# Attention and MLP on one Trainium2 core: a new order for the first batch of attention heads, another order of its loads, and the last result in two halves

## The chip, the cores and the metric

The kernel runs on one core of one Trainium2 chip. The metric is device time in microseconds (us) of one execution. Most numbers below are medians of several runs; the profile of one run gives the span (first to last instruction, some 1.7 us shorter than the time). The runs here are called slow when they are over 1.5% above the fastest of the same kernel, and the others fast.

## The reference, cut to what matters

```python
batch, n_heads, seq, head_dim = 8, 8, 576, 64
scores = q @ k.T / sqrt(64);  cum = cumsum(max(s, 0))
scores = where(causal, -1e9, scores + min(-(cum_i - cum_j), 0))
attn   = softmax(scores)
x      = (attn @ v) as [4608 tokens, 512]        # all heads of a token side by side
h      = x @ w_in                                 # 512 -> 2048
out    = (h * clip(h + 3, 0, 6) / 6) @ w_out      # 2048 -> 512, fp32 out
```

Nothing of the MLP for a batch can start before all eight heads of that batch are through. So the first batch, heads 0 to 7 (pairs 0 to 3), stands alone at the start of the kernel; every later batch is woven into the MLP of an earlier one.

## The kernel before: the parts that matter

In the traces, TensorE's matmuls and VectorE's instructions stand in the order in which the program issues them: in one pass before, VectorE's copies, division, cast of v and next copies start at 25.48, 26.51, 27.50 and 28.16 us. The work of a pair of heads goes round the engines like this (cuts are marked):

```python
def transpose_group(p, g):              # q and k of pair p: PE transposes, then VectorE
    ...                                 # 5 or 4 PE transposes into one PSUM bank
    for dst, r0 in ((qT, 0), (kT, 64)):
        nc.vector.tensor_copy(out=dst[...], in_=pT[...])           # L262
def cast_v(p):                          # on VectorE for p < 4
    copy(out=v_h[:, sl, :, :, 0:D], in_=v_f[:, sl])                # L238
def scores_bank(hd, bi):                # four banks a head
    nc.tensor.matmul(out=S, lhsT=kT[...], rhs=qT[...])             # L291
    nc.scalar.activation(out=P, in_=S, func=AF.Exp)                # L299
    nc.gpsimd.affine_select(...)        # causal mask                L304
def attend(hd):                         # "values"
    nc.tensor.matmul(out=O, lhsT=P[...], rhs=v_h[...])             # L340, 15 of them
    if hh == 1:                         # second head of the pair: divide
        nc.vector.reciprocal(...); nc.vector.tensor_tensor(out=xs, ...)   # L350, L352
def x_transpose(p):                     # output transposes of the pair
    nc.tensor.matmul(out=pX, lhsT=xs[...], rhs=ident, is_transpose=True)  # L378
    nc.vector.tensor_copy(out=xT[...], in_=pX)                     # L386
```

The order of the first batch before (one pass per pair p):

```python
scores(2p)
if p == 1: cast_v(0); load_v(3); load_aug(3); ...; attend(0)
transpose_group(p + 1, 0)               # p < 3
attend(2p - 1)                          # p > 0
scores(2p + 1)
cast_v(p)                               # p > 0
cast_qk(p + 2)                          # p < 2, on GpSimd
transpose_group(p + 1, 1)
x_transpose(p - 1); attend(2p)          # p > 0
... after the last pass: keep_warm(4); attend(7); x_transpose(3); first projection (L423)
```

The softmax here doesn't subtract the row's maximum and nothing guards it: scores larger than these inputs give would overflow.

## Time and profile before

| | before |
|---|---|
| median time | 376.63 us of 3 runs (375.51 to 377.32) |
| span of the profiled run | 374.9 us, mean granted clock 0.994 |
| first projection starts | 35.56 us |
| last matmul ends | 370.86 us (367.24 + 3.62) |

The first projection splits the kernel: up to there the engines hand small pieces to one another, after it TensorE is nearly full (busy 327.87 of the 335.30 us to the end of the last matmul).

### The profile page before, as it was taken

What the parts mean: (1) busy time and instruction counts of PE and PEld (TensorE: products, weight loads), DVE (VectorE), ACT (ScalarE), POOL (GpSimd) and SP (SyncE); (2) the same over time, 40 slices, a digit from 0 to 9 for tenths busy, and PEclk for the clock granted to TensorE, in tenths of its full rate; (3) what the DMA queues carried; (4) which work ended last, traced back from release to release, by engine and by line L of the source; (5) the groups of instructions that cost most, each with busy time, mean ns of one, the idle gap of its engine ahead of it and who ended that gap; (6) DMA issues with size and microseconds to landing.
All of it is one profiled execution on the core that took longest, in us unless ns stands there. A gap on an engine that the chain in (4) does not pass through costs nothing.

```text
span 374.9 us, 7607 instructions
## 1 busy us (share of the span) xinstructions
PE 354.1 (94%) x2784; PEld 219.6 (59%) x2784; DVE 190.9 (51%) x331; ACT 209.5 (56%) x404; POOL 148.9 (40%) x378
## 2 busy tenths in 40 slices
PE   6688979999999999999999999999999999999995
PEld 2465555556666566566656665666566656555542
DVE  5765855566652365345534553455345545554531
ACT  4464764336785677467746774677467714543310
POOL 5663335453666444444444444444445300000000
PEclk9989999999999999999999999999999999999999
DMA  9679999949799999998998989899995100010012
GB/s 161 138 155 203 191 212 211 229 118 194 147 205 204 231 219 198 202 235 189 187 235 180 199 183 233 191 191 185 219 188 113 49 29 36 22 56 30 28 58 84
DMA packets 184526, 59.36 MB, mean 158 GB/s; under 512 B 177840, under 2 KB 178064, under 8 KB 184488
## 3 DMA queue, kind: packets, MB, share of 16 engines
q1 hardware_dynamic: 182392, 54.42, 69.5%
q0 software_dynamic: 1680, 4.27, 6.3%
q8 instruction: 22, 0.36, 0.4%
q10 hardware_dynamic: 416, 0.19, 0.2%
q14 instruction: 16, 0.13, 0.1%
HBM read 37.49 MB, written 9.62 MB: 126 GB/s over the span
## 4 chain that ended last, share of the span: by engine, by line
PE 79%; DMA 8%; DVE 5%; ACT 4%; issue 2%; SPq 1%; POOL 1%; ACTq 0%; POOLq 0%
PE bank L423 25%; PE po L445 23%; PE S L291 9%; PE bank L445 8%; PE O L340 6%; PE bankS L423 4%; DMA qkT<-xb 3%; DMA qkT<-aug_scratch 3%; ACT Pm L299 2%; DMA qkf<-in_k_dram 1%; ACT trl L431 1%; DVE gT L432 1%; PE bank L465 1%; DMA s_sb<-in_s_dram 1%; DVE xs L352 1%
## 5 line engine op out<-in xcount | busy, mean ns | idle before, releaser
L299 ACT ACTIVATE Pm<-S 128x384 f16<-128x384 f32 (+2 forms) x256 | 115.5, 507 | 58.8 <-PE S L291 57.1
L432 DVE SCALAR_TENSOR_TENSOR gT<-trl,bank 128x512 f16<-128x512 f32 x123 | 84.5, 687 | 102.2 <-ACT trl L431 102.0
L304 POOL TENSOR_SCALAR_AFFINE_SELECT Pm<-Pm 128x128 f16<-128x128 f16 (+2 forms) x256 | 79.2, 311 | 132.6 <-ACT Pm L299 121.9
L431 ACT ACTIVATE trl<-bank,bias 128x512 f32<-128x512 f32 x123 | 85.2, 693 | 77.3 <-PE bank L423 75.3
L423 PE MATMUL bank<-xT,w_in 128*128 128x512 f16 x492 | 126.4, 382 | 0.7
L445 PE MATMUL po<-w_out_sb,gT 128*128 128x512 f16 x416 | 104.3, 379 | 0.0
L423 PEld LDWEIGHTS <-w_in 128*128 128x128 f16 x576 | 78.5, 146 | 32.9 <-issue 1.9
L445 PEld LDWEIGHTS <-gT 128*128 128x128 f16 x576 | 52.2, 98 | 48.6 <-issue 0.3
L291 PE MATMUL S<-qkT 128*128 128x320 f16 (+4 forms) x448 | 70.4, 263 | 8.0 <-ACT Pm L299 3.4
L291 PEld LDWEIGHTS <-qkT 128*128 128x128 f16 x448 | 41.3, 98 | 38.4 <-DVE qkT L262 4.5
L340 PEld LDWEIGHTS <-Pm 128*128 128x128 f16 x960 | 38.9, 98 | 13.2 <-POOL Pm L304 1.8
L340 PE MATMUL O<-v_h,Pm 128*128 128x65 f16 x960 | 41.4, 194 | 1.5 <-POOL Pm L304 1.3
L445 PE MATMUL bank<-w_out_sb,gT 128*128 128x512 f16 x160 | 39.4, 379 | 0.0
L352 DVE TENSOR_TENSOR xs<-O,r 128x640 f16<-128x640 f32 x32 | 26.4, 825 | 1.1
L454 DVE TENSOR_SCALAR osb<-po 128x512 f32<-128x512 f32 x26 | 17.9, 688 | 15.2 <-PE po L445 14.9
L222 POOL CAST xb<-qkf 128x1152 f16<-128x1152 f32 x22 | 25.3, 1149 | 0.0
L238 POOL CAST v_h<-v_f 128x640 f16<-128x640 f32 x28 | 20.1, 719 | 4.2 <-DMA v_f<-in_v_dram 4.2
L454 DVE TENSOR_SCALAR osb<-bank 128x512 f32<-128x512 f32 x10 | 6.9, 690 | 26.0 <-PE bank L445 26.0
L176 POOL CAST t<-qkf 128x1152 f16<-128x1152 f32 x10 | 11.5, 1146 | 13.1 <-DMA qkf<-in_k_dram 13.1
L423 PE MATMUL bankS<-xT,w_in 128*128 128x512 f16 x64 | 16.4, 379 | 0.0
L431 ACT ACTIVATE trl<-bankS,bias 128x512 f32<-128x512 f32 x16 | 11.0, 687 | 8.0 <-PE bankS L423 8.0
L432 DVE SCALAR_TENSOR_TENSOR gT<-trl,bankS 128x512 f16<-128x512 f32 x16 | 11.0, 689 | 6.8 <-ACT trl L431 6.8
(49 smaller groups left out, 122.7 us busy)
## 6 DMA issues: line engine op xcount, KB each, us to landing
qkf<-in_q_dram SPq DMA_DIRECT2D x32, 288.0 KB, 4.4
qkf<-in_k_dram SPq DMA_DIRECT2D x32, 288.0 KB, 4.1
out_dram<-osb SPq DMA_DIRECT2D x36, 256.0 KB, 2.7
v_f<-in_v_dram SPq DMA_DIRECT2D x64, 128.0 KB, 3.8
w_in<-in_moe_w_in_dram POOLq DMA_DIRECT2D x2, 1024.0 KB, 12.9
w_out_sb<-in_moe_w_out_dram POOLq DMA_DIRECT2D x4, 512.0 KB, 7.2
v_f<-in_v_dram SPq DMA_DIRECT2D x32, 32.0 KB, 2.7
qkT<-xb SPq DMA_TRANSPOSE x22, 4.9
```

What stands on the lines that cost most here:

```text
L222: nc.gpsimd.tensor_copy(out=x.rearrange("p (i t) c -> p t i c", i=2)[:, :, :, 0:D], in_=qk_f.pop(p))
L238: copy(out=v_h[:, sl, :, :, 0:D], in_=v_f[:, sl])
L291: nc.tensor.matmul(out=S[:, c:c + hi - lo], lhsT=kT[:, sl, off + 128 * kt:off + 128 * (kt + 1)], rhs=qT[:, sl, off + lo:off + hi], start=( ...
L299: nc.scalar.activation(out=P[:, p0:p0 + n], in_=S[:, 0:n], func=AF.Exp, scale=0.125, bias=0.0)
L304: nc.gpsimd.affine_select(out=view, in_=view, pattern=pattern, compare_op=ALU.is_ge, fill=0.0, base=0, channel_multiplier=-1,)
L340: nc.tensor.matmul(out=O[:, hh, qt * VW:qt * VW + D + 1], lhsT=P[:, c:c + 128], rhs=v_h[:, sl, hh, kt, 0:D + 1], start=(qt == 0), stop=(qt ...
L352: nc.vector.tensor_tensor(out=xs.rearrange("p t h d -> p h t d"), in0=Ov[:, :, :, 0:D], in1=r.to_broadcast([128, 2, 5, D]), op=ALU.mult,)
L423: nc.tensor.matmul(out=ph, lhsT=w_in_t[f // 8][:, kc, f % 8, :], rhs=xT[:, kc, n * 512:(n + 1) * 512], start=(kc == 0), stop=(kc == KC - 1),)
L431: nc.scalar.activation(out=trl, in_=ph, func=AF.Relu, bias=bias3[:, 0:1], scale=1.0)
L432: nc.vector.scalar_tensor_tensor(out=gT[n][:, f, :], in0=trl, scalar=6.0, in1=ph, op0=ALU.min, op1=ALU.mult)
L445: nc.tensor.matmul(out=po, lhsT=gT[n][:, f, t4 * 128:(t4 + 1) * 128], rhs=w_out_sb[:, f, :], start=(f == 0), stop=(f == NF - 1),)
L454: nc.vector.tensor_scalar_mul(out=osb, in0=po, scalar1=1.0 / 6.0)
```

## The change

Its intent: values two heads behind the scores, so that TensorE never waits for the causal masks; both groups of transposes of the next pair together; q and k of pair 3 loaded ahead of v of pairs 1 and 2; in each later load the small rows (`load_aug`) first. A second part, outside the first batch, computes the very last 128x512 result in two halves of 256 columns, the second evicted by ScalarE and sent by its queue.

```diff
 def load_pair(p):
+    if p < PTD: load_aug(p, nc.sync)
     load_qk(p, nc.sync); load_v(p, nc.sync)
-    if p < PTD: load_aug(p, nc.sync)
...
+for p in range(4):
+    run(scores(2 * p))
+    if p == 0:
+        transpose_group(1, 0)
+    else:
+        if p < 3:
+            transpose_group(p + 1, 0)
+            transpose_group(p + 1, 1)
+        cast_v(p - 1)
+        ...                                  # p == 1: load_v(3), load_aug(3), store_aug(1)
+        attend(2 * p - 2)
+    run(scores(2 * p + 1))
+    if p == 0:
+        transpose_group(1, 1)
+    else:
+        attend(2 * p - 1)
+        x_transpose(p - 1)
+    ...                                      # cast_qk(p + 2), w_in loads, load_pair(p + 2)
+cast_v(3)
+attend(6)
...
+load_qk(3, nc.sync)
 load_v(1, nc.sync)
+load_v(2, nc.sync)
...
+def last_result(n, t4):                      # replaces the last 128x512 result
+    for half, eng in enumerate((nc.sync, nc.scalar)):
+        ... 16 matmuls of 256 columns, evicted by VectorE (half 0) or ScalarE (half 1),
+        ... eng.dma_start(out=out[...], in_=osb[...])
```

More of the change, by code (lines that the diff above doesn't have):

```diff
@@ L443, in m2 @@
         po = pouts[n, t4]
+        if (n, t4) == (NBLK - 1, 3):
+            if part == 3:
+                last_result(n, t4)
+            return
         for f in range(4 * part, 4 * part + 4):
@@ L456, in m2 @@
             nc.sync.dma_start(out=out[r0:r0 + 128, :], in_=osb)
+    def last_result(n, t4):
+        r0 = n * 512 + t4 * 128
+        osb = work.tile([128, 512], F32, tag="osb", bufs=3)
+        for half, eng in enumerate((nc.sync, nc.scalar)):
+            c0, c1 = half * 256, (half + 1) * 256
+            po = pouts[n, t4] if half == 0 else psum.tile([128, 512], F32, tag="Y", name="poL")
+            for f in range(NF):
+                nc.tensor.matmul(
+                    out=po[:, 0:256],
+                    lhsT=gT[n][:, f, t4 * 128:(t4 + 1) * 128],
+                    rhs=w_out_sb[:, f, c0:c1],
+                    start=(f == 0),
+                    stop=(f == NF - 1),
+                )
+            if half == 0:
+                nc.vector.tensor_scalar_mul(out=osb[:, c0:c1], in0=po[:, 0:256], scalar1=1.0 / 6.0)
+            else:
+                nc.scalar.mul(out=osb[:, c0:c1], in_=po[:, 0:256], mul=1.0 / 6.0)
+            eng.dma_start(out=out[r0:r0 + 128, c0:c1], in_=osb[:, c0:c1])
     bias3 = cpool.tile([128, 1], F32, tag="c_b3")
@@ L492, in load_pair, with first_batch @@
     def load_pair(p):
+        if p < PTD:
+            load_aug(p, nc.sync)
         load_qk(p, nc.sync)
         load_v(p, nc.sync)
-        if p < PTD:
-            load_aug(p, nc.sync)
     def scores(hd):
         return [(lambda bi=bi: scores_bank(hd, bi), 400) for bi in range(4)]
-    def first_tasks(p):
-        def loads():
+    def first_batch():
+        for p in range(4):
+            run(scores(2 * p))
             if p == 0:
-                load_qk(3, nc.sync)
-                load_v(2, nc.sync)
-            elif p > 1:
-                load_pair(p + 2)
-        def v_first():
-            cast_v(0)
-            load_v(3, nc.sync)
-            load_aug(3, nc.sync)
-            store_aug(1, NA, 2 * PTD, nc.sync)
-        def casts():
-            if p > 0:
-                cast_v(p)
+                transpose_group(1, 0)
[4 more added lines that the diff above has]
+                cast_v(p - 1)
+                if p == 1:
+                    load_v(3, nc.sync)
+                    load_aug(3, nc.sync)
+                    store_aug(1, NA, 2 * PTD, nc.sync)
+                attend(2 * p - 2)
+            run(scores(2 * p + 1))
+            if p == 0:
+                transpose_group(1, 1)
+            else:
+                attend(2 * p - 1)
+                x_transpose(p - 1)
             if p < 2:
@@ L525, in casts @@
                 load_w_in(1)
-        tr = [[], []]
-        if p < 3:
-            tr = [[(lambda: transpose_group(p + 1, 0), 640)],
-                  [(lambda: transpose_group(p + 1, 1), 512)]]
-        t = scores(2 * p)
-        if p == 1:
-            t += [(v_first, 0), (lambda: attend(0), 1200)]
-        t += tr[0]
-        if p > 0:
-            t += [(lambda: attend(2 * p - 1), 1200)]
-        t += scores(2 * p + 1) + [(casts, 0)] + tr[1]
-        if p > 0:
-            t += [(lambda: x_transpose(p - 1), 640)]
-            t += [(lambda: attend(2 * p), 1200)]
-        return [(loads, 0)] + t
+            if p > 1:
+                load_pair(p + 2)
+        cast_v(3)
+        attend(6)
     pause = [(lambda: None, 1000)]
@@ L667 @@
         load_aug(p, nc.sync)
+    load_qk(3, nc.sync)
     load_v(1, nc.sync)
+    load_v(2, nc.sync)
     cast_qk(1)
     keep_warm(12)
-    for p in range(4):
-        run(first_tasks(p))
+    first_batch()
     load_pair(6)
```

## The prediction

> **What bounds the kernel now.** I read first the page's busy rows in 40 slices, to see where TensorE is not full.
>
> ```profile
> PE   6688979999999999999999999999999999999995
> ...
> PEclk9989999999999999999999999999999999999999
> ```
>
> One slice is 374.9 / 40 = 9.4 us. From slice 8 on TensorE is full at the full clock, so work there costs what it costs. The holes are in the first seven slices, some 66 us, and in the last. The rewritten order concerns the "first batch" (heads 0 to 7), so I read TensorE's own timeline next; columns are start, length, work, and in brackets the idle time before it and what ended it.
>
> ```profile
> 17.35 0.71 PE L291 MATMUL S<-qkT 128*128 128x256 f16 x6 [1.56 <-DMA qkT<-aug_scratch]
> 18.25 0.30 PE L291 MATMUL S<-qkT 128*128 128x320 f16 x1 [0.19 <-ACT Pm L299]
> 18.39 0.80 PE L340 MATMUL O<-v_h,Pm 128*128 128x65 f16 x15
> 19.00 0.72 PE L247 MATMUL pTm<-ident,t 128*128 128x128 f16 x5
> 19.52 1.03 PE L340 MATMUL O<-v_h,Pm 128*128 128x65 f16 x15
> ...
> 25.00 0.45 PE L247 MATMUL pTm<-ident,t 128*128 128x128 f16 x5 [0.87 <-POOL t L176]
> ...
> 33.46 0.63 PE L340 MATMUL O<-v_h,Pm 128*128 128x65 f16 x15
> 35.27 0.45 PE L378 MATMUL pT<-ident,xs 128*128 128x128 f16 x5 [1.17 <-DVE xs L352]
> 35.56 1.95 PE L423 MATMUL bank<-xT,w_in 128*128 128x512 f16 x8
> ```
>
> The batch runs from 12.7 us to 35.56 us, where the first projection (L423) begins; from there TensorE has few holes. The start of L423 is therefore what this part of the change moves. TensorE has short waits, each on ScalarE, VectorE or a transfer; none is on the causal masks of GpSimd, which "two heads back" would remove. The exponentials (L299) are 16 + 8 + 8 instructions of 0.50, 0.60 and 0.46 us, 16.5 us for eight heads, and ScalarE sits idle 6.0 us between them. So ScalarE could be a floor, but the handovers are what is paid now.
>
> Third, VectorE's timeline, because values (L340) need its cast of v (L238), scores need its copies of the transposes (L262), and the output transposes (L378) need its division (L350, L352).
>
> ```profile
> 25.48 0.99 DVE L262 COPY qkT<-pTm 64x640 f16<-64x640 f16 x2 [1.82 <-PE pTm L247]
> 26.51 0.22 DVE L350 RECIPROCAL r<-O 128x10 f32<-128x10 f32 x1
> 26.76 0.82 DVE L352 TENSOR_TENSOR xs<-O,r 128x640 f16<-128x640 f32 x1
> 27.50 0.73 DVE L238 CAST v_h<-v_f 128x640 f16<-128x640 f32 x1
> 28.16 0.85 DVE L262 COPY qkT<-pTm 64x512 f16<-64x512 f16 x2
> 29.04 0.46 DVE L386 COPY xT<-pTm 128x576 f16<-128x576 f16 x1
> ```
>
> In the kernel before, only one of the two copy pairs stands ahead of a cast, and the division is covered by scores and transposes.
>
> Fourth, windows of 1 us (the columns I use are TensorE busy and the granted clock).
>
> ```profile
> 19.00:20.00 1.00, 1.00 (x18) 1.00 (x16) 0.24 (x1) 0.40 (x2) 0.59 (x3) 0.50 0.89 205
> 20.00:21.00 1.00, 1.00 (x14) 0.91 (x13) 0.95 (x3) 0.03 (x1) 0.00 (x0) 0.50 1.29 290
> 21.00:22.00 1.00, 1.00 (x8) 0.68 (x6) 0.97 (x3) 1.00 (x3) 0.41 (x1) 0.50 1.18 229
> 22.00:23.00 1.00, 1.00 (x26) 0.99 (x24) 0.94 (x3) 0.70 (x2) 0.84 (x3) 0.96 0.47 98
> ```
>
> After the hole of 1.6 us at 16 us the clock was half from about 18.7 (0.83 in that microsecond) to 22.1.
>
> [...] a matmul that waits for VectorE holds every later matmul, and a cast placed behind four copies waits for all four; the recorded order of both engines here is the program's. [...] the 36 output transfers here landed in 2.0 to 4.1 us (median 2.7), so halving the last one saves little of it.
>
> **The change part by part.** I build the new schedule with the old durations. Blocks on TensorE, from starts in the trace: one head's scores hold it 1.1 us (22.87 to the fourth bank at 23.83 and its 0.13), since the fourth bank waits for an exponential; one head's values 0.47 (32.13 to 32.60); five output transposes 0.28 (35.27 to 35.56).
>
> Part 1, both transposes, then the cast, then values. In the first pass this is scores(2), transposes of pair 2, cast of v 0, values(0). From the first transpose to the first copy 0.48 (25.00 to 25.48), copies 0.99 + 0.85, cast 0.7, and some 0.15 of handovers: 3.16 us until values may start, of which the transposes use 0.5. TensorE stands 2.7 us, twice (passes 1 and 2). Before, the same values started directly, or waited 0.19.
>
> Part 2, output transposes directly after the second head's values. From the start of values to the transpose is 1.81 us (33.46 to 35.27: values 0.47, division and handovers 1.34). TensorE stands 1.3 us, three times. Before, this was covered but for 0.41.
>
> A pass is then 1.1 + 3.16 + 0.47 + 1.1 + 1.81 + 0.28 = 7.92 us. The passes from scores(2) to scores(4) and from there to scores(6) were 5.52 (17.35 to 22.87) and 5.89 (to 28.76). The entry at 17.35 stays: it waits for a transfer that the change leaves in its place. So scores(6) start at 17.35 + 15.84 = 33.2. The last pass has no transposes of q and k: 1.46 until values(4) (the cast of v 2 behind the copy L386), 0.47, scores 1.1, values and division 1.81, output transposes 0.28, then 1.44 for the copy and the cast of v 3 before values(6), 0.47, warm matmuls 0.86, values and division 1.81, transposes 0.28: 10.0 us. L423 starts at 43.2 against 35.56: **+7.6 us**.
>
> Part 3, loads. Pair 3's q and k now arrive earlier, which removes the 0.87 us wait on L176; but in the new order VectorE is later than that, so it is worth nothing in the batch. The small rows go ahead of q and k in each load; TensorE waited 1.13 us for them at 56.60. That should go, also because everything is later while transfers are not: **-1.2 us**.
>
> Part 4, the clock. With holes of 2.7 us the clock should drop in more windows. At half clock one head's values took 0.84 (19.52 to 20.36) and scores 1.37 (20.36 to 21.73). A cold pass costs 2 x 0.37 + 2 x 0.27 + about 0.5 on transposes = 1.8 us. I take a little over one cold pass on the path: **+2.0 us**, between 0.5 and 5.
>
> Part 5, which the short description does not mention: the last 128x512 result in two halves, the second evicted by ScalarE. TensorE's work is the same (32 matmuls of 256 for 16 of 512). The end eviction was 0.69 us on VectorE; ScalarE from PSUM takes 0.60 for 512 columns and 0.46 for 320, so about 0.4 for 256; the transfer is half: **-0.4 us**.
>
> Sum 7.6 - 1.2 + 2.0 - 0.4 = +8.0; 376.6 + 8.0 = 384.6 us.
>
> **The rivals.** (a) The intent works: ScalarE becomes the bound, its 6.0 us of idle falls to its first 1.3, and L423 starts 4 us or so earlier; with the end, about 372. For it: two heads of slack, three score banks. Against: both new waits are on VectorE, and three banks hold at most 1.5 us of ScalarE's work, less than either. (b) The delay is absorbed: transfers ran at a DMA share over 1 from 28 to 40 us and the qk of pair 4 reached GpSimd only at 42.4, so a late start could cost nothing later. Against: after 35.56 the TensorE waits up to 75 us sum to 4.6 us and only 1.13 of them is on a transfer. If half is absorbed: about 380. (c) The clock stays half nearly throughout and into L423: 388 to 390.
>
> **Range and chances.** The two stalls are program order and measured durations, so a slowdown is nearly sure; its size hangs on the clock and on absorption. Predicted 384.6, range 380 to 389. The 2% line is 384.2, nearly at my centre: slower by over 2% 0.54, within 2% 0.44, faster by over 2% 0.02.
>
> **What would show it.** In the changed profile: L340 waiting on L238 about 2.5 us twice, L378 waiting on L352 over 1 us in each pass, ScalarE idle around 12 us in the batch, more windows of clock 0.50, L423 starting at 43 to 46 us, no wait on small rows near 56. Wrong would be: L423 at or before 36 us; or L423 late and the end not late, which would be absorption; or a clock at 1.00 throughout, which would make it about 382.6.

## The result, and the profile after

The changed kernel took 387.05 us (median of 4 runs, 386.08 to 388.62) against 376.07 us (375.51 to 377.32, 4 runs). The ratio of the fast runs is 1.0291, 95% interval 1.0241 to 1.0342: slower. A ratio is the mean time of one kernel's fast runs over that of the other's of the same rounds, so it is not quite the ratio of the medians. The profiled run has a span of 384.5 us.

First the page of the changed kernel, the two rows in 40 slices (counted from 1, each 9.6 us). In slices 2 to 5 TensorE's row reads 7, 5, 7, 6 where it read 6, 8, 8, 9 before, and the clock row falls to 7, 6 and 8 in slices 3 to 5, where before only slice 3 was below 9, at 8.

```profile
PE   6757687999999999999999999999999999999996
PEclk9976899999999999999999999999999999999999
```

Next TensorE's timeline of the changed kernel (start, length, work, idle time before it and its releaser).

```profile
18.35 1.16 PE L247 MATMUL pTm<-ident,t 128*128 128x128 f16 x9
21.56 0.98 PE L340 MATMUL O<-v_h,Pm 128*128 128x65 f16 x15 [2.05 <-DVE v_h L238]
22.36 1.57 PE L291 MATMUL S<-qkT 128*128 128x256 f16 x7
23.72 1.03 PE L340 MATMUL O<-v_h,Pm 128*128 128x65 f16 x15
25.92 0.45 PE L378 MATMUL pTm<-ident,xs 128*128 128x128 f16 x5 [1.17 <-DVE xs L352]
...
30.11 0.62 PE L340 MATMUL O<-v_h,Pm 128*128 128x65 f16 x15 [2.13 <-DVE v_h L238]
...
41.49 0.63 PE L340 MATMUL O<-v_h,Pm 128*128 128x65 f16 x15 [1.04 <-DVE v_h L238]
...
46.11 1.95 PE L423 MATMUL bank<-xT,w_in 128*128 128x512 f16 x8
```

The values wait 2.05, 2.13 and 1.04 us for the cast of v, and each output transpose about 1.17 us for the division. Why the cast is late stands on VectorE's own timeline: it has nothing to do for 2.58 us before 19.12, and v of pair 0 was issued by 14.6 us (in run 6 below, with the same order of loads, its cast starts at 16.69), and yet the cast comes only behind the four copies, because the program put it there. The scores issued behind the waiting values start only after them, at 22.36 us on TensorE's timeline.

```profile
19.12 1.86 DVE L262 COPY qkT<-pTm 64x640 f16<-64x640 f16 x4 [2.58 <-PE pTm L247]
21.01 0.49 DVE L238 CAST v_h<-v_f 128x640 f16<-128x640 f32 x1
```

The first projection starts at 46.11 instead of 35.56 us: **+10.55 us**, and the whole span grew by 9.6. The loss is all in the first batch; the rest of the kernel gained about 1 us. The profiled run is the second fastest of the four; the others had spans of 384.4, 386.2 and 386.9 us at mean clocks of 0.978, 0.973 and 0.965, against 384.5 at 0.976: the lower the clock, the longer the run.

Stretches from head 2's scores to the first projection, one line for each kernel (before, then after); after the engines' busy times comes the granted clock, then the DMA share and GB/s.

```profile
17.30:35.56 18.26, 14.47 (x205) 11.29 (x206) 11.57 (x23) 10.09 (x24) 10.72 (x28) 0.91 0.91 175
```

```profile
17.20:46.10 28.90, 18.26 (x204) 14.14 (x205) 10.88 (x23) 10.28 (x24) 13.72 (x33) 0.70 0.97 184
```

VectorE and ScalarE do the same work, 11 and 10 us; what grew is the stretch around it, at a mean clock of 0.70 instead of 0.91. In the trace the clock is half from 18.1 to 24.9, from 31.8 to 38.6 and from 42.0 to 45.4 us, 17.0 us in all, where the kernel before had 3.4 us (18.7 to 22.1).

### The profile page after: what moved, and what is told of

Same layout as the page of the kernel before. It is cut to its first block, busy times and chain, and to the rows that moved or that the text cites. A ratio compares the mean times of both kernels' runs of the same rounds, so it can differ in the third digit from the quotient of the medians.

```text
span 384.5 us, 7646 instructions
## 1 busy us (share of the span) xinstructions
PE 357.8 (93%) x2800; PEld 224.2 (58%) x2800; DVE 189.4 (49%) x331; ACT 209.8 (55%) x405; POOL 148.1 (39%) x378
## 4 chain that ended last, share of the span: by engine, by line
PE 80%; DVE 6%; ACT 4%; DMA 4%; issue 2%; SPq 1%; POOL 1%; ACTq 0%; POOLq 0%
PE bank L423 25%; PE po L450 22%; PE S L291 11%; PE O L340 7%; PE bank L450 7%; PE bankS L423 4%; ACT Pm L299 3%; DVE qkT L262 2%; DMA qkT<-xb 2%; ACT trl L431 1%; DVE gT L432 1%; DVE xs L352 1%; PE bankY L423 1%; DMA qkT<-aug 1%; DMA s_sb<-in_s_dram 1%
## 5 line engine op out<-in xcount | busy, mean ns | idle before, releaser
L423 PE MATMUL bank<-xT,w_in 128*128 128x512 f16 x492 | 126.4, 382 | 0.7
L423 PEld LDWEIGHTS <-w_in 128*128 128x128 f16 x576 | 78.5, 146 | 33.3 <-issue 2.4
L291 PE MATMUL S<-qkT 128*128 128x320 f16 (+4 forms) x448 | 71.9, 267 | 7.1 <-ACT Pm L299 2.7
L450 PEld LDWEIGHTS <-gT 128*128 128x128 f16 x560 | 50.7, 98 | 46.7 <-issue 0.3
L340 PEld LDWEIGHTS <-Pm 128*128 128x128 f16 x960 | 40.5, 100 | 18.7 <-issue 6.6
L340 PE MATMUL O<-v_h,Pm 128*128 128x65 f16 x960 | 43.0, 198 | 6.5 <-DVE v_h L238 5.2
L450 PE MATMUL bank<-w_out_sb,gT 128*128 128x512 f16 x144 | 35.8, 379 | 0.0
L350 DVE RECIPROCAL r<-O 128x10 f32<-128x10 f32 x32 | 6.9, 216 | 24.3 <-PE O L340 24.3
L423 PE MATMUL bankS<-xT,w_in 128*128 128x512 f16 x64 | 16.4, 379 | 0.0
```

Source lines behind the costliest of these rows:

```text
L291: nc.tensor.matmul(out=S[:, c:c + hi - lo], lhsT=kT[:, sl, off + 128 * kt:off + 128 * (kt + 1)], rhs=qT[:, sl, off + lo:off + hi], start=( ...
L340: nc.tensor.matmul(out=O[:, hh, qt * VW:qt * VW + D + 1], lhsT=P[:, c:c + 128], rhs=v_h[:, sl, hh, kt, 0:D + 1], start=(qt == 0), stop=(qt ...
L423: nc.tensor.matmul(out=ph, lhsT=w_in_t[f // 8][:, kc, f % 8, :], rhs=xT[:, kc, n * 512:(n + 1) * 512], start=(kc == 0), stop=(kc == KC - 1),)
L450: nc.tensor.matmul(out=po, lhsT=gT[n][:, f, t4 * 128:(t4 + 1) * 128], rhs=w_out_sb[:, f, :], start=(f == 0), stop=(f == NF - 1),)
```

## The experiments

Ten kernels ran, in jobs that each ran the kernel before beside them. All gave the correct result.

### 1. The cast ahead of the copies

```diff
+                cast_v(p - 1)
                 if p < 3:
                     transpose_group(p + 1, 0)
                     transpose_group(p + 1, 1)
-                cast_v(p - 1)
```

> The changed kernel with one line moved: in the passes with transposes, the cast of v stands ahead of the four copies in VectorE's queue instead of behind them. Theory (order in VectorE's queue): the waits of TensorE for the cast of 2.05 and 2.13 us in passes 1 and 2 vanish, together with the windows at half clock that they cause; the first projection starts 4 to 6 us earlier than 46.1 us, at 40 to 42, and the time is 381 to 383. Rival (the waits only move, to the output transposes or the scores that need the copies): the first projection starts at 44 or later and the time is 385 or more.

Measured: 380.88 us (379.24 to 381.71, 4 runs) against 375.89 (7 runs), ratio 1.0128 (1.0096 to 1.0159). TensorE's timeline at the same places: the values of head 0 have no wait any more, and the first projection comes at 39.72 us.

```profile
19.41 1.03 PE L340 MATMUL O<-v_h,Pm 128*128 128x65 f16 x15
...
39.72 1.95 PE L423 MATMUL bank<-xT,w_in 128*128 128x512 f16 x8
```

Moving one line recovers 6.4 of the 10.55 us, more than the two waits themselves (4.2 us), because time at half clock went with them: two stretches of 3.4 us in the batch instead of 17.0 us, and the mean clock of the run rose from 0.976 to 0.990. The rival, that the waits only move, falls. It did slightly better than the 381 to 383 us expected.

### 2. Output transposes one block later

`x_transpose(p - 1)` of pairs 0 and 1 moves behind the scores of head 2p + 2:

```diff
 attend(2 * p - 1)
-x_transpose(p - 1)
+if p == 3: x_transpose(2)
...                                          # next pass, behind scores(2p)
+if p > 1: x_transpose(p - 2)
```

> The changed kernel with the output transposes of pairs 0 and 1 put behind the next head's scores, as a cover for VectorE's division; those of pair 2 stay where they are. Theory: two waits of 1.17 us on the division go, 2.3 us, and with some half clock 2 to 3.5 us in all; the time is 383.5 to 385, the first projection at 43 to 44. Rival (the wait for the cast of v behind the copies grows by the copy of the output, 0.46 us a pass, and takes most of it back): within 1 us of the changed kernel.

Measured: 383.99 us (382.98 to 384.76, 4 runs), ratio 1.0214 (1.0193 to 1.0235); first projection at 44.08. The two waits on the division are gone. The first projection is 2.0 us earlier, at the lower end of the 2 to 3.5 us expected; by the medians it is 3.1 us. The waits for the cast of v are now 2.25, 1.78, 0.95 and 1.04 us, the third of them new, since the copy of the output (L386) stands ahead of that cast. So the rival (waits that move) had a part in it.

### 3. Both edits

> Both edits together. Theory (the two orders are the whole loss in the batch): the first projection starts at 36 to 39 us, near the 35.56 us of the kernel before, and the time is 376 to 379. Rival (something else in the change costs too, for instance the order of the loads, or the clock stays half for reasons of its own): 381 or more, with TensorE's waits on VectorE gone.

Measured: two of four runs fast, 379.70 and 379.19 us, ratio 1.0095 (1.0075 to 1.0115); the other two, 385.55 and 385.93 us, are slow, at a mean clock of 0.978 against 0.995. First projection of the profiled (fast) run at 39.57 us: nearly where the first edit alone has it, and not at 36 to 39 as expected. Two things filled the space. TensorE waited 1.87 us for the small rows of pair 3, which this order needs earlier than they are loaded, and still 0.95 and 1.04 us for casts of v behind an output copy. So removing both orders gives back 6.5 of the 10.55 us, 0.15 us more than the first edit alone, because behind them stand the next waits; the theory that they are "the whole loss" falls.

### 4. Fillers in TensorE's holes

The changed kernel, with matmuls on zeros in a free PSUM bank at the five places where TensorE waits: 4 and 8 ahead of the values in passes 1 and 2, 3 ahead of the output transposes of pairs 0 to 2. Useful work, order and the waits on VectorE are unchanged.

```diff
+filler(4 if p == 1 else 8)                  # p < 3
 attend(2 * p - 2)
...
 attend(2 * p - 1)
+filler(3)
 x_transpose(p - 1)
```

> The changed kernel with warm-up matmuls put into the five holes of TensorE (4 and 8 ahead of the values, 3 ahead of each output transpose), in a bank that is free there. They do no useful work; the waits on VectorE stay. Theory (the clock has a share of its own, some 2 to 3 us of the 10.5): the granted clock stays 1.00 after the first window, the first projection starts at 43 to 44.5 us, the time is 384 to 385.5. Rival (the clock only slows work that lies beside VectorE's chain): same clock gain, but the first projection stays at 45.5 to 46.5 and the time is within 1 us of the changed kernel.

Measured: 381.76 us (381.22 to 383.53, 4 runs), ratio 1.0167 (1.0136 to 1.0198). TensorE's timeline and the same stretch as above:

```profile
21.43 0.63 PE L340 MATMUL O<-v_h,Pm 128*128 128x65 f16 x15 [0.48 <-DVE v_h L238]
...
42.05 1.95 PE L423 MATMUL bank<-xT,w_in 128*128 128x512 f16 x8
```

```profile
17.10:42.05 24.95, 19.19 (x225) 12.69 (x226) 10.88 (x23) 10.09 (x24) 10.57 (x29) 0.93 0.97 183
```

The values of head 0 still start at 21.4 us: the handover is as late as before. But the clock in the stretch is 0.93 instead of 0.70 and the first projection comes 4.06 us earlier. This splits the loss in two: some 6.5 us are the handovers themselves (35.56 to 42.05, both kernels with one stretch of 3.4 us at half clock), some 4 us the other 13.6 us at half clock, which are gone once the holes are filled. By the ratios the clock is worth 1.24% of 376, or 4.7 us. The rival, a clock that only slows work beside VectorE's chain, falls; the expectation of the theory (384 to 385.5 us) was too small by half.

### 5. Only the split last result, on the kernel before

> The kernel before with only the split of the last result in two halves. Theory: the time from TensorE's last matmul to the end of the span falls from 4.0 us to 3.5, as in the changed kernel, and nothing else moves: -0.3 to -0.6 us, 375.3 to 375.6. Rival [...]: 0 to +0.3 us.

Measured: 375.98 us (374.90 to 378.93, 4 runs), ratio 0.9994 (0.9941 to 1.0047), too wide to decide half a microsecond. The trace tells it. After TensorE's last matmul (end at 367.83 + 1.91 = 369.74 us) the span runs 3.46 us to 373.2; in the kernel before it is 374.9 - 370.86 = 4.04. The tail is worth 0.6 us. The last eviction took 0.38 us on ScalarE instead of 0.69 on VectorE; the rest, some 0.3 us, is a smaller transfer on another queue, and no run separates the two.

```profile
367.83 1.91 PE L470 MATMUL poL<-w_out_sb,gT 128*128 128x256 f16 x16
...
369.78 0.38 ACT L480 ACTIVATE osb<-poL 128x256 f32<-128x256 f32 x1 [13.17 <-PE poL L470]
```

### 6. Only the order of the loads, on the kernel before

> The kernel before with only the new order of the loads: q and k of pair 3 ahead of v of pairs 1 and 2, and in each later load the small rows first. Theory: the wait of 0.87 us on the cast of q and k goes and the wait of 1.13 us on the small rows of pair 5 goes, but the first projection starts at most 1 us earlier; -0.5 to -1.5 us, 374.4 to 375.4. Rival (what the changed kernel showed: the wait at the small rows is replaced by one on VectorE's copies, so that it is worth 0.4 us or less): 375.5 to 376.2.

Measured: 376.86 us (376.68 to 378.96, 4 runs), ratio 1.0022 (0.9972 to 1.0071): the same, and it lies outside both expected ranges. The two waits did go: TensorE's 0.87 us on the cast of q and k, and its 1.13 us on the small rows. But v of pair 1 now lands later. VectorE, then TensorE:

```profile
22.86 0.54 DVE L238 CAST v_h<-v_f 128x640 f16<-128x640 f32 x1 [1.55 <-DMA v_f<-in_v_dram]
```

```profile
23.45 0.98 PE L340 MATMUL O<-v_h,Pm 128*128 128x65 f16 x15 [1.63 <-DVE v_h L238]
```

The values of head 2 wait 1.63 us, and the first projection starts at 36.21 us. In the changed kernel no cast of v waits for its load, since the casts come later.

### 7. and 8. A better order, and w_in a pass earlier

From the first four runs follows an order: two heads back as in the change, but each cast of v issued ahead of the next scores, output transposes one block later, small rows of pair 3 ahead of its v, and the four warm-up matmuls moved to the wait ahead of the output transposes of pair 2.

```diff
 for p in range(4):
+    if p > 0: cast_v(p - 1)
     run(scores(2 * p))
     ...
+        if p > 1: x_transpose(p - 2)
         transpose_group(p + 1, 0); transpose_group(p + 1, 1)    # p < 3
-        cast_v(p - 1)
         attend(2 * p - 2)
+    if p == 3: cast_v(3)
     run(scores(2 * p + 1))
     ...                                    # load_aug(3) at the end of pass 0
+keep_warm(4); x_transpose(2)
 attend(6)
```

> The changed kernel with an order for the batch that follows from the experiments: values two heads back as it has them, each cast of v ahead of the next scores, output transposes one scores block later, small rows of pair 3 ahead of its v, the warm matmuls in the last hole. Theory (handovers to VectorE are the loss): TensorE is ready for the first projection at 32 to 33 us. Rival (the weights w_in are the next bound: they were issued at 24.9 us and took at least 10.4 us, so they landed at 35.3, just ahead of the first projection at 35.56 in the kernel before): it starts at 34 to 36 us whatever the batch does, with a wait on w_in of 2 us or so, and the time is 374.5 to 376.

Measured: two of four runs fast, 374.86 and 375.12 us, ratio 0.9956 (0.9905 to 1.0006); two slow, 382.18 and 384.44 us, at a mean clock of 0.987 and 0.982 against 0.995 to 1.000. The first projection of the profiled (fast) run starts at 34.46 us, and TensorE did not wait for w_in: the step before it waits 1.18 us for the division, so the rival is not shown. But 32 to 33 us was not reached either; VectorE's cast of v of pair 3 waited 2.06 us for its transfer and held the division of pair 2.

Then the first half of w_in one pass earlier, its issue moved from behind `cast_qk(3)` to behind `cast_qk(2)`:

```diff
+            if p == 0: load_w_in(0)
             if p == 1:
-                load_w_in(0)
                 load_w_in(1)
```

> The same with the first half of w_in issued one pass earlier, after the cast of pair 2. Theory (w_in bounds the run before this one): the first projection starts at 31.5 to 33.5 us, the time is 371.5 to 373.5, better than both kernels. Rival (the early transfer delays q and k of pair 3 and the small rows, so the batch itself is later): the first projection at 34 or later, 374.5 or more.

Measured: 381.51 us (380.63 to 382.57, 4 runs), ratio 1.0130 (1.0091 to 1.0168), first projection at 41.18 us. The rival holds, with v of pair 1 as its victim. VectorE waits 5.07 us for it, and TensorE's second group of transposes, whose bank is freed by a copy behind that cast, waits 4.74 us:

```profile
28.63 0.49 DVE L238 CAST v_h<-v_f 128x640 f16<-128x640 f32 x1 [5.07 <-DMA v_f<-in_v_dram]
```

```profile
29.54 0.58 PE L247 MATMUL pTm<-ident,t 128*128 128x128 f16 x4 [4.74 <-DVE xT L386]
```

The w_in transfer comes from GpSimd's queue and v from SyncE's, and yet v came later: with w_in issued at 17.94 us and under way for 10.0 us or more, the cast of v of pair 1 started at 28.63, 9.8 us after the last issue of that v (18.80); in run 7, with w_in issued at 22.64 us or later, the same cast started at 22.22. How w_in delayed v is not shown.

### 9. and 10. The better order and the kernel before, with the early hole filled

To run 7's kernel: six fillers ahead of head 2's scores (the hole at 16 us), four ahead of the last output transpose, and the cast of v of pair 3 behind the division.

> The better order of the run before the last, with three edits: six warm-up matmuls in the hole of 1.3 us ahead of head 2's scores, four in the hole ahead of the last output transpose, and the cast of v of pair 3 behind the division of pair 2. Theory (that order is fast or slow by the clock alone, 375 against 382 to 384 us, and the clock falls after the hole at 16 us): no run falls to the slow group, the granted clock is 0.998 or more in all runs, 373.5 to 375.5 us in each. Rival (the clock falls for another reason, or from run to run whatever fills that hole): again runs of 380 and over.

Measured, 5 rounds: 375.38 us (373.92 to 381.04, 6 runs) against 375.62 (11 runs), ratio of the fast runs 0.9985 (0.9966 to 1.0004). Five of the six runs had clock 1.000 and took 373.92 to 375.79 us; one was slow, 381.04 us at 0.991. So the theory falls: one run in six was slow, against two in four before, too few to call it rarer, and the kernel differs from run 7's by the moved cast as well. What makes those runs is open, since only fast runs' traces of these orders were kept. In the traces the hole at 16 us was 1.27 us in run 5 and 1.33 in run 7, and the clock stayed full; in the kernel before it was 1.56 us, and the clock fell to half at 18.7. In the profiled run the first projection starts at 33.94 us and the span is 372.2. Against the kernel before it is the same: no version here is shown to beat it.

The kernel before, with the six fillers ahead of head 2's scores and nothing else:

> The kernel before with only the six warm-up matmuls ahead of head 2's scores. Theory (one window of half clock after that hole costs this kernel its scatter, 375.5 to 378): clock 1.00 and 375.3 to 376 in all runs, scatter under 0.7. Rival: scatter as without, medians equal within 0.3 us.

Measured, 5 rounds: 376.57 us (375.55 to 379.89, 6 runs), ratio 1.0042 (1.0010 to 1.0074). The clock in the profiled run's batch is 1.00 throughout, and yet the time is not lower: the theory falls, and the scatter stayed. In the profiled runs the one stretch at half clock costs the kernel before some 0.5 us between head 2's scores and the first projection: 18.21 us with it (17.35 to 35.56), 17.78 in run 5, whose batch is the same and whose clock stayed full (16.93 to 34.71), and 17.67 with the fillers (17.21 to 34.88). Run 5, then the run with fillers:

```profile
34.71 1.95 PE L423 MATMUL bank<-xT,w_in 128*128 128x512 f16 x8
```

```profile
34.88 1.95 PE L423 MATMUL bank<-xT,w_in 128*128 128x512 f16 x8
```

Over whole runs it is not clear. Among the 11 runs of the kernel before in this job, those at a clock of 0.993 took 375.96 and 375.61 us, and four at 1.000 took 374.79 to 375.94. But in the job of runs 5 to 8 the three at 0.993 to 0.995 took 377.24 to 377.96 us, and the four at 0.998 to 1.000 took 375.55 to 375.89. Why the fillers made the kernel 0.4% slower stays open.

## Why the prediction was right

The range (380 to 389 us) holds the measured 387.05, and "slower by over 2%", the likeliest of its three, came true with 2.9%. There is some luck in this: the handovers were put 1.1 us too high and the clock 2.1 us too low, and with the clock at its predicted size the spans would have grown by some 7.5 us, which is 2.0%, the line itself. Its terms, beside what the runs showed:

| step of the prediction | predicted | measured | from |
|---|---|---|---|
| handovers to VectorE | +7.6 | +6.5 | first projection 35.56 to 42.05, with fillers (run 4) |
| clock | +2.0 | +4.1 | 42.05 to 46.11, without fillers |
| small rows, rest of the kernel | -1.2 | -0.4 | first projection to last matmul's end, 335.30 to 334.92 |
| last result in halves | -0.4 | -0.6 | last matmul's end to end of span, 4.04 to 3.47 |
| sum | +8.0 | +9.6 | spans 374.9 to 384.5 |

**Handovers.** The mechanism was right wait by wait: about 2.7 us twice was expected for the cast behind the copies and 2.05 and 2.13 came, 1.3 us for the division and 1.17 came. Runs 1 and 2 removed the two orders separately and the time came back both times. The term is 1.1 us too large. Some 0.7 us of it (an estimate, three times 0.22) is the cast of v, which was put at 0.7 us, near its median of 0.64 in the kernel before, and took 0.48 or 0.49 in the changed kernel; another 0.27 is that run 4's batch entered head 2's scores at 17.08 us and not at 17.35. The list of waits before has one slip that changes no sum: the 0.87 us wait at 25.00 is for GpSimd's cast of q and k (L176), and not for ScalarE, VectorE or a transfer. L423 came at 46.11 us, at the edge of the 43 to 46 named as a sign.

**Clock.** This term was mis-sized by half: "a little over one cold pass" is 2.0 us, and the runs showed 17.0 us at half clock and 4.1 us on the path. That the clock would fall in more places was the estimate from the one hole of 1.56 us in the trace before. The step at fault is the time at half clock, which was not worked through; the range given for it, 0.5 to 5, holds the result. With 3.4 us of it left (run 4) the whole change would have been 1.7%, not 2.9.

**Loads.** That the earlier q and k of pair 3 are worth nothing in the new order fits the trace, and no run tests it alone; but run 6 shows that they are not free either: alone, they make the values of head 2 wait 1.63 us for v. The gain of 1.13 us at the small rows of pair 5 was counted whole. That wait did go, but two on VectorE, 0.91 us together, stand in its place. TensorE before, and then after, at the same scores:

```profile
56.60 0.54 PE L291 MATMUL S<-qkT 128*128 128x256 f16 x4 [1.13 <-DMA qkT<-aug_scratch]
```

```profile
66.78 0.72 PE L291 MATMUL S<-qkT 128*128 128x192 f16 x4 [0.55 <-DVE qkT L262]
67.86 0.30 PE L291 MATMUL S<-qkT 128*128 128x320 f16 x1 [0.36 <-DVE xT L386]
```

**Last result.** The mechanism was right for the eviction (0.38 us on ScalarE in run 5, about 0.4 predicted), and the whole was 0.6 us for 0.4. That halving the transfer saves little of its time was the estimate: the 2.0 to 4.1 us are whole transfers of 256 KB, no landing time of a half stands in the traces, and run 5 does not separate transfer and queue. For comparison, the transfers of v in the kernel before took a median of 2.7 us for 32 KB and 3.8 for 128 KB.

**Rivals.** Rival (a), ScalarE as the bound, did not come: ScalarE's idle time between exponentials in the batch rose from 6.0 to 12.3 us. Rival (b), absorption, is at most part of the 0.4 us of the third row. Rival (c), the clock, has come in part: half clock for 17 of the 29 us of the batch, but full again at the first projection.

The median rose by 11.0 us and the spans by 9.6, because the profiled run of the changed kernel (386.20 us) is one of its two faster ones and that of the kernel before (376.62 us) is above its median.

## What to carry to other kernels

When work is reordered on one engine, write down the order that results on the engines that serve it: here a cast of 0.5 us was put behind copies of 1.9 us in VectorE's queue, and TensorE waited 2.05 and 2.13 us for it. A hole in TensorE can cost twice, once itself and once by the clock that falls after it, here some 6.5 us for the handovers and some 4 for the clock; fillers in the hole separate the two in one run. And try each part of a change alone: of the three here, the split result was worth 0.6 us, the loads nothing, and the new order, by what is left, lost over 10.

## The clock in these traces

- The full clock was lost after gaps of 1.56 us (kernel before, at 16 us), of 1.57 and 2.13 us, and of 1.18 and 1.04 us close together (changed kernel). It was kept after gaps of 1.27 us in run 5 and 1.33 us in run 7, both at 16 us, and of 1.17 us at 25.9 us in the changed kernel.
- In the 3.4 us just ahead of a fall of the clock TensorE was busy 1.64 us (before), and 1.60, 1.44 and 1.18 us (after). From 24.95 to 28.40 us in the changed kernel it was busy 1.80 of 3.45 us, and from 22.08 to 35.7 us in the kernel before 2.23 to 3.01 of each 3.4 us, and the clock stayed full. Two of the changed kernel's three stretches at half clock lasted 6.8 us, with TensorE busy 1.38 and 2.23 of their first 3.4 us; the third lasted 3.4 us with 2.65 busy, and that of the kernel before 3.4 us with TensorE busy throughout.
- The changed kernel had 13.6 us more at half clock than run 4. An estimate from the clock alone, half of that time, is 6.8 us; the first projection moved by 4.1 us. The 3.4 us of the kernel before would by the same estimate cost 1.7 us and cost some 0.5. In both TensorE also waits for other engines, and how much of the loss such waits hide is not shown.
